# A decode kernel that streams its K and V: V beside a row's chain in halves, the row's kept K after eight of these V instead of sixteen, q spread at the chain's end

## The chip, the core and the metric

The kernel runs on one core of a Trainium2 chip. The metric is the device time of one execution in microseconds; below it is the median of three runs. One more execution was recorded by the hardware profiler, and all views of the profile are of that one.

## What is computed

A batch of 8 rows, one token each, 448 wide, goes twice through the same two blocks: an attention over a cache, then a small MLP. Both passes use the same weights and the same caches.

```
x = x + A(layernorm(x));  x = x + B(layernorm(x))     # pass 0
x = x + A(layernorm(x));  x = x + B(layernorm(x))     # pass 1

A(x):  q = x @ wq                    # 16 heads of 256; 8 heads of K and V, two q heads to each
       p = softmax(q k^T / 16)       # k, v: [8 rows, 8 heads, 4096, 256] bf16, read from HBM
       return (p v) @ wo
B(x):  h = gelu(layernorm(x) @ w1) ; shift by 1 or 2 tokens ; x1 = x + hs @ w2
       return x1 + gelu(layernorm(x1) @ w3) @ w4
```

With one token, the shift in B leaves zeros, so the product with w2 adds nothing, and the kernel leaves w1 and w2 out. K and V have 134 MB each, and each pass needs both; the second pass of a row needs its q, which depends on the whole first pass of that row.

## The kernel before

**Tiles and places.** Work on a row (batch element) is cut into four tasks, one for each pair of K/V heads (`gp` 0 to 3), and each task into four K chunks and four V chunks of 1 MB. A chunk lies in one of 15 places in SBUF (`NC = 15`, L61): 128 partitions of 8 KB, sixteen rows of 256 values in each. A task of pass `ps`, row `b` and heads `gp` is written `(ps, b, gp)` in the code, and an item is a task, 0 or 1 for K or V, and a chunk number.

**Kept chunks.** Chunks that both passes of a row use are kept where possible (`kept`, L64): for the heads in `keep` (gp 2 and 3), all eight K chunks (already transposed by pass 0) and four V chunks stay in their places from pass 0 to pass 1 of the row; one more V chunk (`inner`) and a quarter of another (`part`) wait in PSUM. So while a row stands between its two passes, twelve of the fifteen places are taken, and three are free to stream through.

**Per chunk.** A K chunk is transposed by VectorE (`transpose_k`, L751) and then scored on TensorE (`scores`, L766; two chunks of a pair are scored together when the first comes up, if they are in place); ScalarE makes the exponentials of two chunks (`exps`, L775). `transpose_p` (L802) and `spread_p` (L900) bring them into the form that PV wants. A V chunk takes 16 matmuls (`pv`, L819), one for each of the 16 rows y of a partition; they read the place in the order of y, so the first eight read its first half.

**The chain.** When the last V of a row's pass 0 has been used, what follows for that row is a chain of small dependent steps (`chain`, L494): copy o out of PSUM (`half`, L467), turn it (L473), product with wo (L365), norm (L227 to L302, with matmul L235 and a power on GpSimd, L254), product with w3 (L383), gelu (L400 to L405), product with w4 (L365), norm, product with wq (L316), q (L325). A chain is a Python generator; each `yield` is a place at which other work may be put. `step(idx)` takes the next piece of every open chain. It is called ahead of an item's matmuls and behind them, and for V of the tasks in `saved` once more between the eighth and the ninth matmul (`between`).

**Spread.** Before K of a row can be scored, its q has to be spread into one of two block-diagonal tiles (`spread_q`: four matmuls L335, four casts L339). That is done when the first K item of a row and pass comes up and no tile holds its q.

**Order.** All instructions are issued in the order of a list of items that `block` and `first_kept` (L553, L569) write by hand before anything is emitted. `due` holds V items that are owed; each K item is followed by one of them. Around a chain the list reads: the row's last kept heads in pass 0; then the V of the saved tasks (`units`), by themselves, while the chain of the row goes on; then K of the row's pass 1, kept heads first. For the first six chains there are four saved tasks, so sixteen V; for the last two only two, so eight V.

**Loads.** `emit_loads` (L698) runs behind every item. It takes the next chunk of `loads` (the items in order, without those that are kept) as long as a place is free, and issues one DMA on SP's queue: 1 MB at L738, or two neighbouring K chunks as 2 MB at L713. SP issues in order; each DMA waits until the place's last reader is done (PE for V, PE for K that has been scored). The very last chunk is the only one that comes in two halves (L741).

Of the kernel before, what the change touches and what calls it, by code (L numbers as in the profile page):

```python
# [17 lines left out]
def kernel(  # L18
# [161 lines left out]
    qbds = [consts.tile([128, 8, GP, 4, 2], BF16, name=f"qbd{k}") for k in range(2)]  # L180
    for t in qbds:
        nc.vector.memset(t[:].rearrange("p n g a h -> p (n g a h)"), 0.0)
    q_of = [None] * len(qbds)
# [144 lines left out]
    def spread_q(qT, qbd):  # L328


        qs = misc[0:32, 128 : 128 + 4 * NB2].rearrange("p (e n) -> p e n", e=4)
        for ep in range(4):
            e2, par = ep // 2, ep % 2
            sel = identb[:, 64 * e2 : 64 * e2 + 64].rearrange("p (j r) -> p r j", r=2)[:, par, :]
            nc.tensor.matmul(qs[:, ep, :], sel, qT, start=True, stop=True)  # L335
        yield
        for a in range(4):
            u = a // 2
            nc.vector.tensor_copy(  # L339
                qbd[32 * a : 32 * a + 32, :, :, a, :],  # L340
                qs.rearrange("p e (f g u h) -> p (e f) u g h", f=2, u=2, h=2)[:, :, u],
            )
# [151 lines left out]
    def chain(b, st, ready):  # L494
        OT = work.tile([128, 2, Hq // 2, 1], BF16, tag="OTb", bufs=1)
        yield from half(st["o", 1], st["z"], 1, OT[:, :, :, 0], ready)
        yield from add_cols(
            y_room(1)[:, 1],
            lambda i: OT[:, i % 2, i // 2 - Hq // 2],
            wo_sb,  # L500
            range(NB2 // 2, NB2),
            2,
        )
        xs = xT[:, :, b : b + 1]
        nc.vector.tensor_add(xs, xs, y_room(1)[:, 1])
        yield from mlp(b, 1)
        qT = chn.tile([128, NB2], BF16, tag="qT2", bufs=2)
        yield from project_q(b, 1, qT[:].unsqueeze(2))
        state[1, b] = {"qT": qT}

    def first_last(b, st, ready):

# [35 lines left out]
        ahead.append(units)  # L548

    tasks, items, due = [], [], []  # L550
    number = {}

    def block(k, v=None):  # L553

        fresh = [(number[v], 1, c) for c in range(4)] if v else []
        if k is None:
            items.extend(due + fresh)
            due.clear()
            return
        number[k] = len(tasks)  # L560
        tasks.append(k)
        for c in range(4):
            items.append((number[k], 0, c))
            items.extend(due[:1])
            del due[:1]
            if c == 0:
                due.extend(fresh)

    def first_kept(b, units, before):  # L569

        k2, k3 = ((0, b, gp) for gp in keep)
        todo = list(units)
        block(todo.pop(0), before)
        if len(todo) > 2:
            block(todo.pop(0))
        block(k2)
        block(todo.pop(0), k2) if todo else block(None, k2)
        block(k3)
        block(todo.pop(0), k3) if todo else block(None, k3)
        assert not todo  # L580
        for u in units:
            block(None, u)

    block((0, 0, free[0]))
    block((0, 0, free[1]), (0, 0, free[0]))
# [112 lines left out]
    def emit_loads(most=None):  # L698
        n = 0
        while loads and places and n != most:  # L700
            it = loads[0]
            both = both_for(it)
            if both:
                p, mate = both
                if p not in places or p + 1 not in places:
                    break
                for i, q in ((it, p), (mate, p + 1)):
                    loads.remove(i)
                    places.remove(q)
                    del held[i]  # L710
                    taken(i, q)
                _, b, gp = tasks[it[0]]
                nc.sync.dma_start(  # L713
                    places_t[:, p * PB : (p + 2) * PB],
                    A_k_cache[b, 2 * gp : 2 * gp + 2]
                    .rearrange("g s d -> (g s) d")
                    .rearrange("(p u z) d -> u p (z d)", u=2, z=32)[it[2] // 2],
                )
                n += 1
                continue  # L720
            p = place_for(it)
            if p is None:
                break
            del loads[0]
            taken(it, p)
            t, kv, c = it
            _, b, gp = tasks[t]
            dst = slots[p]
            rows = (A_v_cache if kv else A_k_cache)[b, 2 * gp : 2 * gp + 2].rearrange(
                "g s d -> (g s) d"  # L730
            )
            if kv:
                src = rows.rearrange("(a p y) d -> a p (y d)", a=4, y=16)[c]
            else:
                src = rows.rearrange("(p x y) d -> x p (y d)", x=4, y=16)[c]
            if loads:
                z0 = Q4 if tasks[t][0] == 1 and halfway(it) else 0
                nc.sync.dma_start(dst[:, z0:], src[:, z0:])  # L738
            else:
                for y in range(2):  # L740
                    nc.sync.dma_start(  # L741
                        dst[:, 8 * Dh * y : 8 * Dh * (y + 1)], src[:, 8 * Dh * y : 8 * Dh * (y + 1)]
                    )
            n += 1
# [117 lines left out]
    def run(g):  # L862
        while True:
            try:
                next(g)
            except StopIteration as e:
                return e.value
# [6 lines left out]
    def step(idx):  # L874

        for kind in ("chain", "last", "rest"):
            e = next((e for e in gens if e["kind"] == kind), None)
            if e is None:
                continue
            if not e["of"] or e["n"] < e["of"] * (idx - e["at"] + 1) / max(e["until"] - e["at"], 1):  # L880
                e["n"] += 1
                if next(e["g"], gens) is gens:
                    gens.remove(e)

    free_slots = list(range(NP))
    slot_of, ring_of = {}, {}
    v_items = [it for it in items if it[1] == 1]
# [16 lines left out]
    for idx, it in enumerate(items):  # L904
# [17 lines left out]
        if kv == 0:  # L922
# [5 lines left out]
                    state[0, b] = {}  # L928
            st = state[ps, b]
            if (ps, b) not in q_of:  # L930

                def next_use(k):
                    return next((m for m in range(n, len(tasks)) if tasks[m][:2] == q_of[k]), 999)

                k = max(range(len(qbds)), key=next_use)
                q_of[k] = (ps, b)
                run(spread_q(st["qT"][:] if ps == 1 else qT1[:, :, b], qbds[k]))
            qbd = qbds[q_of.index((ps, b))]
            if "z" not in st:
                z_t = chn.tile([128, 2, GP], FP32, tag="zall", bufs=4)  # L940
# [29 lines left out]
        else:  # L970
# [9 lines left out]
            if final and gp in free:  # L980
                pv_cols(oc, slot, c, gp, psv[slot_of[n]])
                if c % 2 == 1:

                    u = c // 2
                    scale_o(oc, rz_gp, gp, u, OT2[:, :, :, b])
                    h0 = 8 * gp + 4 * u
                    run(
                        add_cols(
                            st["y"],
                            lambda i: OT2[:, i % 2, i // 2, MID:],  # L990
                            wo_sb,
                            range(h0, h0 + 4),
                            4,
                            open=(claim(st), gp == free[-1] and u == 1),
                        )
                    )
            else:
                g8 = gp // 2
                if ("o", g8) not in st:
                    while len(in_use) == 2:  # L1000
                        step(10 * len(items))
                    st["o", g8] = next(t for t in o_banks if all(t is not u for u in in_use))
                    in_use.append(st["o", g8])
                if c == 0 and pairs_done.get((ps, b), 0) % 2 == 1:
                    done = pairs_done[ps, b] + 1

                    def ready(k=(ps, b), done=done):
                        return pairs_done[k] >= done

                    if ps == 0:  # L1010
                        g = (first_half if done == 2 else chain)(b, st, ready)
                        add_gen("chain", g)
                    elif done == 2:
                        add_gen("chain" if final else "last", first_last(b, st, ready))
                    else:
                        add_gen("last", last(b, st, ready))
                calm = tasks[n] in saved
                pv(st["o", g8], slot, c, gp, ring_of[it], (lambda: step(idx)) if calm else None)
                if ps == 0 and inside(it):
                    away(slot)  # L1020
                if ps == 0 and halfway(it):
                    nc.vector.transpose(store[4][:].bitcast(U32), slot[:, 0:Q4].bitcast(U32))
# [83 lines left out]
```

## Time and profile before

| | |
|---|---|
| median of three runs | 1136.0 us (1134.33 to 1137.39) |
| the profiled execution | 1138.53 us, span 1136.7 us |
| DMA | 438.25 MB, mean 386 GB/s |
| PE matmul busy | 652.4 us (57%) |
| DVE busy | 605.1 us (53%) |
| ACT busy | 164.0 us (14%) |
| PV, L819 | 3968 matmuls, 236.8 us |
| scores, L766 | 5376 matmuls, 252.2 us |
| transposes of K, L751 | 576, 457.7 us |
| V loads of 1,024 KB | 207, median 8.8 us from issue to landing |

PE is TensorE, DVE VectorE, ACT ScalarE, POOL GpSimd, SP the engine that issues the DMAs; "SPq" is its queue. The slices of the profile are fortieths of the span, 28.4 us each. A wait line names who waited and for whom, then the total in us, how often, and the longest. A timeline line gives start and length in us, engine, line and operation, and in brackets the idle time ahead of it and what ended that. "The chain that ended last" in the profile is the path of waits that led to the last instruction; it is not the row's chain of the section above.

### The profile page before, as it was taken

How to read it: one execution, taken by the hardware profiler on the slowest of the kernel's cores; microseconds unless marked ns; L12 is line 12 of the kernel's file. 1: busy time of each engine (PE TensorE's matmuls, PEld its weight loads, DVE VectorE, ACT ScalarE, POOL GpSimd, SP SyncE). 2: the span in 40 equal slices, each digit the busy share in tenths (PEclk: the TensorE clock that was granted, in tenths of full speed). 3: DMA queues.
4: the chain of work that ended last, by engine and by line, in shares of the span. 5: the costliest groups of instructions: out<-in, count | busy, mean ns of one | idle time of the engine just before them, and what ended most of it. 6: DMA issues, size and time to landing. Idle time of an engine off the chain costs nothing.

```text
span 1136.7 us, 30536 instructions
## 1 busy us (share of the span) xinstructions
PE 652.4 (57%) x13748; PEld 421.3 (37%) x13748; DVE 605.1 (53%) x1242; ACT 164.0 (14%) x610; POOL 16.3 (1%) x27
## 2 busy tenths in 40 slices
PE   3234476734757357564575555664466646865875
PEld 2122244512434235332353323442243424543654
DVE  4248730687306972268623685138741574476272
ACT  0011110211102111121101211011110111111020
POOL 0000000000000000000000000000000000000000
PEclk9985555756556555565555655556555655566565
DMA  9999999999999999899998999999999799999994
GB/s 357 397 424 428 423 392 340 368 425 417 365 365 397 423 396 364 326 427 421 419 337 321 428 423 409 359 356 428 421 402 362 313 423 418 348 424 421 358 396 200
DMA packets 56386, 438.25 MB, mean 386 GB/s; under 512 B 5944, under 2 KB 9920, under 8 KB 11712
## 3 DMA queue, kind: packets, MB, share of 16 engines
q1 hardware_dynamic: 56064, 435.93, 95.5%
q8 instruction: 107, 1.75, 0.6%
q10 hardware_dynamic: 192, 0.38, 0.1%
q14 instruction: 23, 0.19, 0.0%
HBM read 436.28 MB, written 0.01 MB: 384 GB/s over the span
## 4 chain that ended last, share of the span: by engine, by line
DMA 54%; PE 23%; DVE 15%; SPq 3%; issue 2%; ACT 1%; POOL 1%; DVEq 0%; ACTq 0%
DMA places<-in_A_v_cache_dram 35%; DMA places<-in_A_k_cache_dram 19%; DVE places L751 11%; PE sc L766 9%; PE o L819 7%; PE misc L365 3%; SPq L174 2%; PE misc L316 2%; DVE store L786 1%; PE misc L473 1%; DVE qbd L339 1%; SPq L738 1%; ACT p_n L775 1%; DMA wq_sb<-in_A_wq_dram 1%; POOL t L254 1%
## 5 line engine op out<-in xcount | busy, mean ns | idle before, releaser
L751 DVE STREAM_TRANSPOSE places<-places 128x512 uint32<-128x512 uint32 (+1 forms) x576 | 457.7, 854 | 100.0 <-DMA places<-in_A_k_cache_dram 98.2
L766 PE MATMUL sc<-places,qbd 128*8 128x128 bf16 (+1 forms) x5376 | 252.2, 339 | 247.0 <-DVE places L751 227.9
L819 PE MATMUL o<-places,ptw 128*8 128x256 bf16 x3968 | 236.8, 384 | 176.9 <-DMA places<-in_A_v_cache_dram 142.3
L766 PEld LDWEIGHTS <-qbd 128*8 128x8 bf16 x5376 | 135.2, 104 | 324.2 <-DVE places L751 163.7
L819 PEld LDWEIGHTS <-ptw 128*8 128x8 bf16 x3968 | 105.8, 104 | 246.1 <-issue 148.3
L775 ACT ACTIVATE p_n<-sc 128x256 bf16<-128x256 f32 x128 | 94.8, 741 | 369.5 <-PE sc L766 369.5
L900 ACT COPY ptw<-psv 128x32 bf16<-128x32 bf16 x248 | 50.9, 225 | 216.9 <-PE o L819 215.7
L468 DVE MEMSET o<- 128x256 f32 x31 | 8.4, 272 | 96.8 <-ACT o_sb L467 52.6
L440 DVE RECIPROCAL rz<-misc 128x8 f32<-128x8 f32 (+1 forms) x33 | 6.6, 201 | 97.2 <-PE misc L437 82.6
L809 ACT CAST psv<-misc 128x128 bf16<-128x128 f32 x64 | 17.0, 265 | 242.4 <-PE misc L802 239.8
L316 PEld LDWEIGHTS <-wq_sb 128*128 128x128 bf16 x1152 | 33.9, 104 | 26.5 <-issue 16.8
L473 PE MATMUL misc<-R,o_sb 128*128 128x8 f32 x124 | 28.7, 342 | 23.7 <-DVE qbd L339 13.3
L365 PEld LDWEIGHTS <-wo_sb 128*128 128x128 bf16 x1280 | 36.9, 104 | 10.3 <-issue 10.2
L473 PEld LDWEIGHTS misc<-R,o_sb 128*128 128x128 f32 x124 | 26.1, 292 | 33.9 <-ACT o_sb L467 19.9
L316 PE MATMUL misc<-xb,wq_sb 128*128 128x1 bf16 x1024 | 31.9, 166 | 7.0 <-DVE xb L283 6.8
L775 ACT ACTIVATION_READ_ACCUMULATOR p_n<-sc 128x1 f32 x128 | 33.7, 263 | 0.0
L254 POOL TENSOR_TENSOR t<-t,nhalf 128x2 f32<-128x2 f32 (+2 forms) x20 | 14.0, 703 | 1108.2 <-DVE t L275 1108.2
L365 PE MATMUL misc<-OT,wo_sb 128*128 128x1 bf16 x1024 | 29.8, 166 | 0.0
L339 DVE CAST qbd<-misc 32x64 bf16<-32x64 f32 x92 | 19.7, 214 | 16.5 <-PE misc L335 15.6
L793 DVE STREAM_TRANSPOSE places<-store 128x512 uint32<-128x512 uint32 x32 | 20.1, 685 | 12.0 <-PE sc L766 12.0
L467 ACT COPY o_sb<-o 128x256 f32<-128x256 f32 x31 | 11.5, 372 | 95.9 <-PE o L819 95.9
L325 DVE CAST qT<-misc 128x32 bf16<-128x32 f32 x8 | 1.5, 192 | 39.2 <-PE misc L316 39.2
(104 smaller groups left out, 308.3 us busy)
## 6 DMA issues: line engine op xcount, KB each, us to landing
places<-in_A_v_cache_dram SPq DMA_DIRECT2D x207, 1024.0 KB, 8.8
places<-in_A_k_cache_dram SPq DMA_DIRECT2D x54, 2048.0 KB, 20.5
places<-in_A_k_cache_dram SPq DMA_DIRECT2D x84, 1024.0 KB, 12.3
places<-in_A_v_cache_dram SPq DMA_DIRECT2D x8, 768.0 KB, 6.3
wo_sb<-in_A_wo_dram SPq DMA_DIRECT2D x1, 3584.0 KB, 28.4
wq_sb<-in_A_wq_dram SPq DMA_DIRECT2D x3, 1024.0 KB, 8.6
w_sb<-in_B_w_dram SPq DMA_DIRECT2D x1, 1568.0 KB
w_sb<-in_B_w_dram SPq DMA_DIRECT2D x3, 448.0 KB, 18.9
```

The source lines that it names most:

```text
L174: nc.sync.dma_start(t[:, fc * cols : (fc + 1) * cols], src[fc * 128 : fc * 128 + 128, :])
L254: nc.gpsimd.tensor_tensor(rs[:, k0:k1].rearrange("p n b -> p (n b)"), ve[:, k0:k1].rearrange("p n b -> p (n b)"), nhalf[:].to_broadcast([1 ...
L316: nc.tensor.matmul(q_ps[:, j * Hq + h, :], w, xbs(nb)[:, xi, :], start=(fc == 0), stop=(fc == 3),)
L339: nc.vector.tensor_copy(qbd[32 * a : 32 * a + 32, :, :, a, :], qs.rearrange("p e (f g u h) -> p (e f) u g h", f=2, u=2, h=2)[:, :, u],)
L365: nc.tensor.matmul(y_ps[:, fc, :], w[:, i, at : at + 128], rhs(i), start=start, stop=stop, skip_group_check=open is not None,)
L473: nc.tensor.matmul(ot_ps[:, j], o_sb[:].rearrange("p (i j) -> p j i", j=2)[:, j], R[:], start=True, stop=True)
L751: nc.vector.transpose(w, w)
L766: nc.tensor.matmul(sc[32 * k : 32 * k + 8, 128 * x : 128 * (x + nx)], qbd[:, ep, gp].rearrange("p a h -> p (a h)"), v, start=(n == 0), sto ...
L775: nc.scalar.activation(p_sb[:, :, :, 2 * u : 2 * u + 2].rearrange("p t i x -> p x t i"), sc[:, 256 * u : 256 * u + 256].rearrange("p (x t ...
L793: nc.vector.transpose(slot[:].bitcast(U32)[:, 512 * n : 512 * n + 512], store[n][:].bitcast(U32))
L819: nc.tensor.matmul(o_ps[32 * q : 32 * q + 8, :], ptz[:, at : at + 8], v[:, y * Dh : (y + 1) * Dh], start=False, stop=(y >= 12), skip_group ...
L900: nc.scalar.copy(ptw[:, ring_of[it], :, 6:8], psv[slot_of[it[0]]][:, it[2]])
```

## The change

Three things are done. In `first_kept`, the V of the saved tasks no longer stand by themselves: they are put into `due`, the first eight (`AFTER`) follow at once, and the rest alternate with the K items that come next, which are the kept K of the row's pass 1. The first eleven of these V are `narrow`: their load is issued as two DMAs of 512 KB, one for each half of the place, and between the eighth and ninth matmul of their PV two steps of the chain are taken; other V take none there any more. And `chain` ends with `give_q`, which spreads the row's new q at once, into the tile whose q is used again latest, counted from the next K item.

```diff
@@ chain
         yield from project_q(b, 1, qT[:].unsqueeze(2))
         state[1, b] = {"qT": qT}
+        give_q((1, b))
@@ the list of items
-    number = {}
+    number, narrow = {}, set()
+    AFTER = 8
     def block(k, v=None):
         fresh = [(number[v], 1, c) for c in range(4)] if v else []
         if k is None:
-            items.extend(due + fresh)
+            due.extend(fresh)
+            items.extend(due)
             due.clear()
             return
@@ first_kept
         assert not todo
+        items.extend(due)
+        due.clear()
         for u in units:
-            block(None, u)
+            due.extend((number[u], 1, c) for c in range(4))
+        narrow.update(due[: AFTER + 3])
+        items.extend(due[:AFTER])
+        del due[:AFTER]
@@ emit_loads
-            if loads:
+            if loads and it not in narrow:
                 z0 = Q4 if tasks[t][0] == 1 and halfway(it) else 0
                 nc.sync.dma_start(dst[:, z0:], src[:, z0:])
             else:
                 for y in range(2):
                     nc.sync.dma_start(
                         dst[:, 8 * Dh * y : 8 * Dh * (y + 1)], src[:, 8 * Dh * y : 8 * Dh * (y + 1)]
                     )
@@ behind step
+    def give_q(who):
+        here = next((i[0] for i in items[now[0] :] if i[1] == 0), 0)
+        def next_use(k):
+            return next((m for m in range(here, len(tasks)) if tasks[m][:2] == q_of[k]), 999)
+        k = max(range(len(qbds)), key=next_use)
+        q_of[k] = who
+        run(spread_q(state[who]["qT"][:] if who[0] == 1 else qT1[:, :, who[1]], qbds[k]))
@@ the loop over items, K
             if (ps, b) not in q_of:
-                def next_use(k):
-                    return next((m for m in range(n, len(tasks)) if tasks[m][:2] == q_of[k]), 999)
-                k = max(range(len(qbds)), key=next_use)
-                q_of[k] = (ps, b)
-                run(spread_q(st["qT"][:] if ps == 1 else qT1[:, :, b], qbds[k]))
+                give_q((ps, b))
@@ the loop over items, V
-                calm = tasks[n] in saved
-                pv(st["o", g8], slot, c, gp, ring_of[it], (lambda: step(idx)) if calm else None)
+                pv(st["o", g8], slot, c, gp, ring_of[it],
+                    (lambda: (step(idx), step(idx))) if it in narrow else None)
```

More of the change, by code (lines that the diff above doesn't have):

```diff
@@ L1016 @@
                         add_gen("last", last(b, st, ready))
-                calm = tasks[n] in saved
-                pv(st["o", g8], slot, c, gp, ring_of[it], (lambda: step(idx)) if calm else None)
+                pv(
+                    st["o", g8],
+                    slot,
+                    c,
+                    gp,
+                    ring_of[it],
+                    (lambda: (step(idx), step(idx))) if it in narrow else None,
+                )
                 if ps == 0 and inside(it):
```

## The prediction

> **What bounds it now.** I read the page's forty slices first, then the shares of the chain that ended last, then the waits of SP's queue, then the stages around one row's chain in the windows view.
>
> ```profile
> PE   3234476734757357564575555664466646865875
> ...
> DMA  9999999999999999899998999999999799999994
> GB/s 357 397 424 428 423 392 340 368 425 417 365 365 397 423 396 364 326 427 421 419 337 321 428 423 409 359 356 428 421 402 362 313 423 418 348 424 421 358 396 200
> ...
> DMA 54%; PE 23%; DVE 15%; SPq 3%; issue 2%; ACT 1%; POOL 1%; DVEq 0%; ACTq 0%
> ```
>
> The DMA row says nine tenths nearly everywhere, but the rate swings between about 425 and 320 GB/s, in dips that come once per row. So the kernel is bound by its transfers (438.25 MB), and the time to be won is in the dips. Windows, with columns length, busy us (count) of PE, weight load, DVE, ACT, POOL, then clock, DMA share and GB/s:
>
> ```profile
> 429.20:452.30 23.10, 19.01 (x434) 14.17 (x438) 5.47 (x32) 2.21 (x10) 1.25 (x2) 0.50 0.96 354
> 452.30:477.00 24.70, 11.60 (x162) 6.95 (x150) 2.23 (x11) 2.34 (x10) 0.00 (x0) 0.50 0.95 367
> 477.00:487.00 10.00, 8.22 (x209) 5.70 (x212) 7.98 (x13) 2.61 (x9) 0.00 (x0) 0.50 0.71 274
> 900.00:950.00 50.00, 25.17 (x538) 14.58 (x530) 37.12 (x56) 8.14 (x30) 0.00 (x0) 0.60 1.01 423
> ```
>
> The last line is a K stretch without trouble: 423 GB/s, which I take as full rate. The first is a row's chain, from the copy of its last o (L467) to its q (L325): PE is busy 19 of 23 us, and 23.1 x (1 - 354/423) = 3.8 us of transfer are lost. The second is the rest of the sixteen V: PE is busy less than half, nothing else works, and still 3.3 us are lost. The third begins at the first score of the kept K: 3.5 us lost.
>
> Why the V stretch loses, with PE idle, is in the waits of SP's queue and in PE's timeline (start, length, what, idle before it):
>
> ```profile
> SPq L738 <- DMA places<-in_A_v_cache_dram: 195.1, 121, 7.0
> SPq L738 <- PE o L819: 167.3, 123, 3.8
> SPq L738 <- PE sc L766: 153.9, 59, 9.3
> ```
> ```profile
> 447.09 1.16 PE L316 MATMUL misc<-xb,wq_sb 128*128 128x1 bf16 x32 [1.00 <-DVE xb L283]
> 448.18 0.60 PE L819 MATMUL o<-places,ptw 128*8 128x256 bf16 x8
> ...
> 473.32 1.02 PE L819 MATMUL o<-places,ptw 128*8 128x256 bf16 x16 [2.49 <-DMA places<-in_A_v_cache_dram]
> 474.13 0.31 PE L335 MATMUL misc<-qT,identb 128*32 128x32 bf16 x4
> 476.10 0.99 PE L473 MATMUL misc<-R,o_sb 128*128 128x8 f32 x4 [1.66 <-DVE qbd L339]
> 477.02 1.88 PE L766 MATMUL sc<-places,qbd 128*8 128x256 bf16 x32
> ```
>
> Twelve of the fifteen places hold what pass 1 will use again, so V runs through three places, and SP can ask for V n+3 only when PV has read V n. PE waits for V, V waits for SP, SP waits for PE: a ring with three members. Then, at 474, the kept K wait for q to be spread (L335, four casts L339, PE idle 1.66), and only their scores free further places: the 3.5 us hole.
>
> Lost per stage, by length x (1 - rate/423) from the same view: for the six rows with sixteen V, chains 2.8, 4.2, 3.8, 3.2, 2.9, 2.8 (sum 19.5; 22.0 to 24.4 us long); rest of V 5.1, 3.3, 3.3, 6.0, 4.4, 3.6 (25.7); first 10 us of kept K 1.8, 1.9, 3.5, 3.4, 2.2, 5.8 (18.6). That is **10.6 us a row, 7.4 of it behind the chain**. The two rows with eight V (chains from 959.6 and 1052.8) lose 2.2 + 3.0 and 3.4 + 2.7.
>
> **The change, part by part.** Sums go against the profiled execution (span 1136.7, time 1138.53, 2.5 above the median of the runs, 1136.0); I take the difference from the median.
>
> *Kept K after eight V.* Nothing is added or removed: the order of V is the same, and eight kept K items move in front of the last eight V of six rows, alternating with them. Each pair of kept K scored frees two places (1.88 us of PE per pair of scores, no transfer, no transpose), so from there on places are freed at twice the rate. The ring of three is opened, and the last eight V (a transfer each of 1,024 KB, 2.5 us at 423 GB/s) are asked for well ahead. On SP these requests stand in the order in which places come free; the first after the narrow V waits for one pair of scores and one PV. The last narrow V is asked for some 25 us after the chain's start, the next request comes about 4.5 us later (half() L473 1.0 with 0.5 of waiting, scores 1.9, PV 1.0), while three V in flight are 7.4 us of work and a request needs about 2 us to flow (issue at 479.02, the 4-us stretch after it back at full rate from 481). So the 7.4 us fall to between 0 and 3; I take 1.0, since transfers end on their slowest queue and not all together. If that cover is gone (PE later by over 3 us), each us is lost once per row, 6 us in all.
>
> *q spread at the chain's end.* Four matmuls (0.31) and four casts (0.88) move out of the stretch where PE idles 1.66 us for them into the V; there the next PV covers the casts. It is part of the 3.5 us hole and is not counted twice. The number of spreads stays 23.
>
> *Halves and the chain.* Now three steps of the chain per V (before it, between its eighth and ninth matmul, after it); then four, two of them in the middle. By the new order PE alternates one PV half, one piece of chain, with twelve halves (six V) up to the spread, where 7.5 V stand in the 23.1 us now. Pieces, from PE's timeline: L473 1.02, L365 1.86, L235 0.59, L383 1.80, L365 1.81, L235 0.56, L437 0.60, L316 about 3.9: 12.1. Twelve halves at 0.55 (0.60 alone, 1.02 the two): 6.6. Waits, each less the half that covers it: copy of o 0.5; end of L365 to L235 0.9 - 0.55 = 0.35; L235 to L383 1.8 - 0.55 = 1.25 (DVE, then POOL 0.70, then DVE); L383 to L365 1.1 - 0.55 = 0.55; again 0.25; L235 to L316 2.0 - 0.55 = 1.4: 4.3. **Sum 23.0, what it is now**: the waits for V (0.66, 1.26, 0.61 in the row shown) go, but a half hides less of DVE's and POOL's latency than a whole PV. The last two V add 2.1 and the spread 0.3: 25.4 us for eight V. DMA meanwhile: what was asked for before the chain lasts until 435.5, that is 6.3 us; twelve halves at 1.27 are 15.2. Lost 25.4 - 21.5 = 3.9, and writing the refills out one by one, each 2 us behind its half, the uneven requests (long gaps at the two norms) make it 4.7. Bounds: 2 if the refill of the first half gains more than a piece of chain, 8 if the chain takes 3 us more. So the chain's own loss does not fall: 3.3 now, **4.7 then**. The gain is all behind it.
>
> *The price of halves.* 6 x 11 + 2 x 8 = 82 V are split: 82 more requests (0.33 us each on SP, which is waiting anyway) and packets of 4,096 B for 8,192. In the packet records of before the last V, the one split today, has 256 packets of median 159 ns; an 8,192 B packet takes 309. So 8 x (318 - 309) = 0.07 us a V, 0.8 a row. Above, 0.7 us a half if each began on an idle queue (packets after a pause take about 1,000 ns); below nothing. I take 0.8, as requests overlap in a ring of six.
>
> The Trainium skill speaks against this part: "DMA: Bandwidth & Descriptors", sections "Measured" and "Rules for kernel authors", asks for at least 1 MiB per transfer, and its fit (section "Anatomy of one DMA") puts about 2.0 us on each transfer whatever its size; an estimate from that page would be 82 x 2 = 164 us more if nothing overlapped. The trace has 1 MiB transfers in a row at 423 GB/s, so the fixed part is covered with several in flight.
>
> *PV without a step in the middle* for the other V: moves pieces of work by one PV, in stretches where PE waits for DMA; nothing. Weight loads fall by 288 pairs (nine more pairs of chunks lie side by side), beside other work: nothing.
>
> *Sum.* Row with sixteen V: 4.7 + 0.8 + 1.0 = 6.5 for 10.6, so -4.1; six rows -24.6. Row with eight: 4.7 + 0.6 + 0.8 = 6.1 for 5.65 on average; two rows +0.9. Together -24: **1112 us**.
>
> **Rivals.**
> (A) *Little gain.* The chain with two pieces between halves runs 2 us longer and DMA starves through it: 6.7 + 0.8 + 2 = 9.5 a row: -6.6, +7: about 1135. For it: PE is busy 19 of 23 us, at a granted clock of 0.50. Against: PE's waits for V vanish.
> (B) *Halves also mend the chain.* Requests half a V earlier keep DMA going: 2 + 0.8 + 0.5 = 3.3 a row, -44, and -5: 1088. For: SP's 167 us of waiting for PE o. Against: PE's own 23 us.
> (C) *Slower.* Place: the narrow V. Mechanism: each half is a transfer of its own and starts late on queues that have run dry, 0.35 us a half (half of the 0.7 above). 164 x 0.35 = 57 us: 1169. It decides from 24/164 = 0.15 us a half. For: starts after a pause are seen all through the dips. Against: six in flight.
> (D) *The halves do nothing*, because a refill waits for the whole PV. The built program's waits say otherwise: a half's refill waits for the eighth matmul.
>
> **Chances.** Forecast (1098 to 1125) 0.62, A 0.15, B 0.14, C 0.08, D 0.01. The range takes in B and most of the way to A: 1089 to 1131. A measurement of this kernel tells 0.3% (3.4 us) from no change: faster 0.87, same 0.05, slower 0.08.
>
> **What will show it.** Windows behind the chains at 400 GB/s and more, and the slices' dips half as long; the chains still 22 to 24 us with a lower rate than now (about 340); no 1.66 us before L473 after the casts of qbd; half V transfers landing in under 8 us. Wrong if the chain windows exceed 25 us, if the K stretches after it fall below 415 GB/s, or if the SP waits for half V grow past what the whole V cost.

## The result, and the profile after

The changed kernel takes 1128.15 us (median of four runs, 1127.98 to 1129.88) against 1136.22 us (median of four runs of the kernel before): a ratio of 0.9934, interval 0.9917 to 0.9951. It is faster by 8 us, a third of the 24 that were forecast; the time lies inside the range, near its slow end. The profiled execution has a span of 1126.2 us for 1136.7.

The same parts of the page as shown of before, now of the changed kernel (slices of 28.2 us, then the shares of the chain that ended last, then the V transfers with count, size and median time to landing):

```profile
GB/s 360 396 425 427 423 363 331 421 425 419 344 366 425 422 412 337 402 424 423 404 325 424 425 425 389 333 426 423 422 355 352 422 422 377 333 425 416 302 420 202
...
DMA 63%; PE 20%; DVE 9%; SPq 3%; issue 2%; POOL 1%; ACT 1%; DVEq 0%; ACTq 0%
...
places<-in_A_v_cache_dram SPq DMA_DIRECT2D x125, 1024.0 KB, 18.0
...
places<-in_A_v_cache_dram SPq DMA_DIRECT2D x166, 512.0 KB, 6.8
```

The dips are narrower and just as deep: in the six long rows their lowest slices are 331, 344, 337, 325, 333 and 352, where 340, 365, 326, 321, 356 and 313 stood. In the two rows with eight V they are deeper, 333 and 302 for 348 and 358. Next the windows view of the changed kernel, one long row (a row with sixteen V: chain, then up to the first kept K, then 12 us from there) and then the first row with eight V, cut alike:

```profile
425.60:447.90 22.30, 17.70 (x410) 12.69 (x411) 5.61 (x32) 1.70 (x8) 1.25 (x2) 0.55 0.92 337
447.90:451.50 3.60, 3.11 (x52) 2.45 (x47) 1.17 (x6) 0.82 (x3) 0.00 (x0) 0.50 0.86 313
451.50:463.50 12.00, 7.21 (x181) 4.29 (x180) 2.95 (x7) 2.55 (x9) 0.00 (x0) 0.78 1.00 379
944.50:967.00 22.50, 18.15 (x410) 12.99 (x411) 5.63 (x32) 1.65 (x8) 1.25 (x2) 0.50 0.86 303
967.00:970.60 3.60, 3.11 (x52) 2.45 (x48) 1.16 (x6) 0.59 (x2) 0.00 (x0) 0.50 0.65 198
970.60:982.60 12.00, 9.38 (x201) 5.95 (x204) 8.20 (x12) 3.50 (x12) 0.00 (x0) 0.50 0.99 406
```

The 25 us of V by themselves are gone: 3.6 us stand between chain and first kept K. But the chain, about as long as before, has fallen from 354 to 337 GB/s, and in the row with eight V from 380 to 303, with 198 behind it. The chain of that row before:

```profile
959.60:981.10 21.50, 19.03 (x434) 14.14 (x438) 5.47 (x32) 2.02 (x9) 1.25 (x2) 0.50 0.99 380
```

SP's waits in the changed kernel (L749 asks for halves, L746 for whole chunks):

```profile
SPq L749 <- PE o L827: 137.0, 101, 2.8
...
SPq L746 <- PE sc L774: 79.3, 33, 3.8
...
SPq L746 <- DMA places<-in_A_v_cache_dram: 68.4, 42, 4.0
SPq L746 <- PE o L827: 42.1, 44, 5.1
...
SPq L749 <- DMA places<-in_A_v_cache_dram: 27.9, 19, 4.7
```

Waiting for earlier V to land fell from 195 to 96 us (68.4 and 27.9); waiting for PE's PV, 167 before, is 179 now (137.0 and 42.1). So PE's PV is now the wait that holds most of the V requests back.

For the comparisons below I count the lost time from the packet records: each packet of 4, 8 and 16 KB at its usual duration (159, 309 and 611 ns, within 3 ns of the medians), smaller ones by their size, summed and divided by sixteen queues, taken off the length of a stretch. That keeps the dearer small packets out of it. For before it gives 3.4 (chain), 4.3 (to the first kept K) and 3.3 (12 us from there) in a mean long row.

| run | us | V in the chain | chain | to K | 12 us from K | long row | rows with eight V |
|---|---|---|---|---|---|---|---|
| before | 1136.2 | 7.5 | 3.4 | 4.3 | 3.3 | 10.9 | 5.4, 6.3 |
| the change | 1128.2 | 6 | 4.6 | 1.2 | 1.6 | 7.3 | 8.5, 7.8 |
| e1 order only | 1114.3 | 7.5 | 3.0 | 1.1 | 3.3 | 7.3 | 5.3, 7.5 |
| e2 old order | 1148.4 | 6 | 4.7 | 3.8 | 2.8 | 11.3 | 7.3, 7.6 |
| e3 one step | 1102.5 | 7.5 | 1.0 | 0.6 | 3.3 | 4.9 | 4.0, 4.4 |
| e4 whole loads | 1127.2 | 6 | 6.1 | 1.8 | 0.7 | 8.6 | 8.3, 9.1 |
| e5 two in the middle | 1109.6 | 7.5 | 1.8 | 0.4 | 3.2 | 5.4 | 5.4, 5.5 |
| e6 one step, late q | 1107.4 | 7.5 | 1.7 | 0.5 | 3.4 | 5.6 | 3.7, 4.3 |
| e7 one step, whole | 1110.6 | 7.5 | 2.9 | 0.7 | 3.1 | 6.7 | 4.8, 8.5 |
| e8 long rows alone | 1121.8 | 6 | 4.5 | 1.4 | 1.4 | 7.3 | 4.6, 7.3 |
| e9 nine V | 1098.5 | 7.5 | 1.4 | 0.8 | 2.0 | 4.2 | 3.0, 4.2 |
| e10 ten V | 1099.4 | 7.5 | 1.1 | 0.7 | 1.5 | 3.2 | 5.0, 4.4 |
| e11 all in halves | 1110.6 | 7.5 | 1.1 | 0.4 | 4.0 | 5.5 | 3.1, 4.7 |

"V in the chain" is how many PV stand between the copy of o (L467) and q (L325) in a long row. The losses are of each run's one profiled execution, the times medians of four. The whole packet time at the usual durations is about 1030 us before and 6 more with the change. The losses can be summed over the eight rows: with the change they are 17 us less, packets add 6, and the two profiled spans differ by 10.5. A loss can move from one stage of a row to the next, so rows are safer to compare than stages.

Each ratio below is to runs of the kernel before that were made beside it, with medians from 1133.7 to 1137.5 us; for e9, e10 and e11 it was 1137.5.

### The profile page after: what moved, and what is told of

It reads as the page before. It is cut to its first block, busy times and chain, and to the rows that moved or that the text cites. A ratio compares the mean times of both kernels' runs of the same rounds, so it can differ in the third digit from the quotient of the medians.

```text
span 1126.2 us, 30082 instructions
## 1 busy us (share of the span) xinstructions
PE 650.9 (58%) x13460; PEld 418.5 (37%) x13460; DVE 607.6 (54%) x1242; ACT 163.6 (15%) x610; POOL 16.3 (1%) x27
## 4 chain that ended last, share of the span: by engine, by line
DMA 63%; PE 20%; DVE 9%; SPq 3%; issue 2%; POOL 1%; ACT 1%; DVEq 0%; ACTq 0%
DMA places<-in_A_v_cache_dram 40%; DMA places<-in_A_k_cache_dram 22%; PE o L827 6%; PE sc L774 5%; DVE places L759 4%; PE misc L316 3%; PE misc L365 3%; SPq L174 2%; DVE store L794 2%; PE misc L383 1%; POOL t L254 1%; SPq L746 1%; PE misc L235 1%; PE misc L473 1%; DMA wq_sb<-in_A_wq_dram 1%
## 5 line engine op out<-in xcount | busy, mean ns | idle before, releaser
L774 PE MATMUL sc<-places,qbd 128*8 128x256 bf16 (+1 forms) x5088 | 249.7, 349 | 220.0 <-DVE places L759 207.5
L827 PE MATMUL o<-places,ptw 128*8 128x256 bf16 x3968 | 242.8, 381 | 151.2 <-DMA places<-in_A_v_cache_dram 129.0
L774 PEld LDWEIGHTS <-qbd 128*8 128x8 bf16 x5088 | 132.4, 105 | 292.3 <-issue 120.6
L365 PEld LDWEIGHTS <-wo_sb 128*128 128x128 bf16 x1280 | 39.2, 104 | 35.0 <-issue 34.9
L316 PEld LDWEIGHTS <-wq_sb 128*128 128x128 bf16 x1152 | 34.7, 104 | 32.1 <-issue 21.7
L316 PE MATMUL misc<-xb,wq_sb 128*128 128x1 bf16 x1024 | 33.2, 165 | 11.5 <-DVE xb L283 8.9
L473 PE MATMUL misc<-R,o_sb 128*128 128x8 f32 x124 | 28.2, 338 | 19.7 <-ACT o_sb L467 11.9
L473 PEld LDWEIGHTS misc<-R,o_sb 128*128 128x128 f32 x124 | 25.5, 286 | 31.4 <-ACT o_sb L467 22.9
L383 PE MATMUL misc<-xb,w_sb 128*128 128x1 bf16 (+1 forms) x560 | 18.8, 166 | 11.8 <-DVE xb L283 9.4
L383 PEld LDWEIGHTS <-w_sb 128*128 128x128 bf16 x560 | 17.9, 105 | 19.4 <-issue 18.6
```

Source lines behind the costliest of these rows:

```text
L316: nc.tensor.matmul(q_ps[:, j * Hq + h, :], w, xbs(nb)[:, xi, :], start=(fc == 0), stop=(fc == 3),)
L365: nc.tensor.matmul(y_ps[:, fc, :], w[:, i, at : at + 128], rhs(i), start=start, stop=stop, skip_group_check=open is not None,)
L383: nc.tensor.matmul(h_ps[:, c * nb : c * nb + nb], w, xbs(nb)[:, xi, :], start=(fc == 0), stop=(fc == 3),)
L473: nc.tensor.matmul(ot_ps[:, j], o_sb[:].rearrange("p (i j) -> p j i", j=2)[:, j], R[:], start=True, stop=True)
L774: nc.tensor.matmul(sc[32 * k : 32 * k + 8, 128 * x : 128 * (x + nx)], qbd[:, ep, gp].rearrange("p a h -> p (a h)"), v, start=(n == 0), sto ...
L827: nc.tensor.matmul(o_ps[32 * q : 32 * q + 8, :], ptz[:, at : at + 8], v[:, y * Dh : (y + 1) * Dh], start=False, stop=(y >= 12), skip_group ...
```

## The experiments

**e1: the order alone.** Of the change, only the list of items is kept.

```diff
-            if loads and it not in narrow:
+            if loads:
@@ chain
-        give_q((1, b))
@@ pv
-                    (lambda: (step(idx), step(idx))) if it in narrow else None,
+                    (lambda: step(idx)) if tasks[n] in saved else None,
```

> Only the order of the items is that of the change (kept K after eight V); V come whole, one step of the chain stands in the middle of a PV as before, q is spread when the first K comes up. Theory 1 (the order is all of the gain; two steps between halves make PE end fewer V in the chain, the halves cost 6 us of packets and more in the two rows with eight V): chain windows lose 3.3 us as before, the stage behind them 3 to 4 instead of 7.4, the short rows as before: 1110 to 1118 us, faster than the whole change. Theory 2 (the halves are needed to feed the ring of three): 1126 us or more. Theory 3 (the early spread of q is what closes the hole): the hole at the first kept K stays 2 us or more a row, 1124 to 1130.

Measured: 1114.25 us, ratio 0.9824 (0.9810 to 0.9839). The order by itself brings 20 us, near the 24 forecast for the whole change, but by chance: a long row loses 3.0 us in the chain and 3.3 at the kept K, where 4.7 and 1.0 were put. What was added to it took 14 away. Theory 1 holds by the time and by the stretch up to the first kept K, where 1.1 us are lost for 4.3. The 12 us from the first kept K still lose 3.3, as before: the order alone does not close that hole. Halves and the early q do not either, since e3 has both and loses the same 3.3 there.

**e2: the order undone.**

```diff
-        items.extend(due[:AFTER])
-        del due[:AFTER]
+        items.extend(due)
+        due.clear()
```

> The change with its order undone: all sixteen V stand by themselves again, the first eleven in halves, two steps in the middle, q spread early. Theory 1: the V behind the chain lose 3 to 5 us a row again and the hole 2 to 3, and the dearer chain stays: 1134 to 1142 us. Theory 2 (halves bring the gain): 1128 or less. Theory 3 (early q brings it): 1120 to 1128.

Measured: 1148.43 us, 1.0121 (1.0104 to 1.0139). Halves, two steps and early q in the old order are 14 us slower than before, worse than theory 1 said. The windows of this run for the same row, chain and V behind it:

```profile
430.20:452.80 22.60, 18.21 (x410) 13.04 (x411) 5.64 (x32) 1.69 (x8) 1.25 (x2) 0.50 0.91 326
452.80:481.30 28.50, 13.46 (x186) 7.75 (x177) 2.19 (x11) 2.79 (x12) 0.00 (x0) 0.50 0.93 348
```

Both stages are below the 354 and 367 GB/s of before, and the second is 3.8 us longer: ten V stand behind the chain where 8.5 stood.

**e3: one step between the halves.**

```diff
-                    (lambda: (step(idx), step(idx))) if it in narrow else None,
+                    (lambda: step(idx)) if it in narrow else None,
```

> The change with one step of the chain between the halves instead of two. Theory 1 (PE sets the pace in the chain, and two pieces between halves put only six V into it where 7.5 were): the chain stays 22 to 24 us long, 7.5 V in it, its loss falls from 4.6 to about 3 us and the 1.2 us behind it go: 1112 to 1118 us. Rival (the chain is a string of latencies that steps cannot shorten, so one step makes it longer and q late): chain windows 25 us and more, 1126 to 1135.

Measured: 1102.46 us, 0.9717 (0.9702 to 0.9731): one step less in the middle is worth 26 us, more than the 10 to 16 expected. Its windows for the same row and for the row with eight V:

```profile
416.50:439.50 23.00, 18.84 (x434) 13.30 (x438) 5.46 (x32) 2.25 (x10) 1.25 (x2) 0.54 1.01 383
439.50:442.30 2.80, 1.71 (x24) 1.42 (x16) 1.15 (x6) 0.37 (x1) 0.00 (x0) 0.50 0.99 369
442.30:454.30 12.00, 7.60 (x217) 5.02 (x217) 3.07 (x7) 3.52 (x13) 0.00 (x0) 0.86 0.88 313
...
926.00:947.30 21.30, 18.77 (x434) 13.98 (x438) 5.48 (x32) 2.02 (x9) 1.25 (x2) 0.50 1.01 377
```

The second step in the middle did not shorten the chain: in the six long rows it takes 22.1 us on average here and 22.3 in the change. What differs is the count of matmuls, 434 against 410, that is 24 more PV matmuls, 1.5 V. From the chain's start to its end this run asks for 14 halves (at 1.4 to 21.0 us), the change for 11 (at 1.4 to 20.8), and so in all six long rows. Three halves are 3.8 us of transfer, 23 us in six rows if nothing of it were made up later. By the table the change loses 14 us more than this run in the long rows and 8 more in the two rows with eight V: 22 of the 26 measured.

**e4: whole loads, two steps.**

```diff
-            if loads and it not in narrow:
+            if loads:
```

> The change with every V loaded whole, still with two steps in the middle. Theory 1: packets of 4,096 B go (-6 us), but a refill now waits behind two pieces of the chain and the second half: 1.5 to 2 us more lost in each of eight chains: 1132 to 1138 us. Rival (halves are mere cost): 1118 to 1122 us, the short rows back at 5 to 6 us lost.

Measured: 1127.23 us, 0.9932 (0.9915 to 0.9948), the time of the change itself, between the ranges of the two theories and in neither. The chains lose 1.5 us more a row, as theory 1 had it, and the packets 6.6 us less in all; the two cancel. With two steps the halves are worth nothing.

**e5: three steps a V, two of them in the middle.**

```diff
         emit_loads()
-        step(idx)
+        if it not in narrow:
+            step(idx)
```

> The change with two steps between the halves, but none behind a narrow V's item: three steps a V as in the kernel before, two of them in the middle. Theory 1 (what costs is the number of V that PE ends while the chain lasts its fixed 22 us; three steps a V put 7 to 7.5 V there): 1102 to 1109 us, chains losing 1 to 2 us. Rival (two pieces in front of the second half are what delays the refills): 1118 to 1130 us, chains losing over 3 us.

Measured: 1109.61 us, 0.9772 (0.9738 to 0.9807), just above the range of theory 1, far from the rival. Of the 26 us, 19 go with the number of steps per V; 7 more go with their place: with two in the middle the chains lose 1.8 us instead of 1.0.

**e6: one step, q spread late.** The edit of e3, and:

```diff
-        give_q((1, b))
```

> One step between the halves, and q spread only when the first kept K comes up, as before. If the early spread matters, four matmuls and four casts stand again in front of the kept K, about 1.5 us a row in a stretch where DMA runs dry: 1108 to 1115 us against 1102.5. If it is covered (the kept K wait in PE behind half() anyway): within 3 us of 1102.5.

Measured: 1107.41 us, 0.9754 (0.9724 to 0.9785). That is 5 us more than e3, but the intervals of the two just overlap, and the stage that would have to show it (to K, 0.5 for 0.6 us) does not. What the table has instead, 1.7 us for 1.0, lies in the chain, ahead of the spread. Whether the early spread is worth 5 us or nothing stays open.

**e7: one step, whole loads.** The edits of e3 and e4 together.

> One step in the middle, q early, new order, but every V loaded whole. Theory 1: without halves the ring has three members of 1 MB; chains lose 3.0 us as in the run with the order alone instead of 1.0, less 0.8 us of packets a row: 1108 to 1114 us. Rival (halves are mere packet cost): 1096 to 1101 us.

Measured: 1110.63 us, 0.9783 (0.9752 to 0.9814). Chains lose 2.9 us for 1.0: halves are worth 8 us, packets paid, when one step stands in the middle; with two (e4) they were worth nothing. Theory 1 holds.

**e8: rows with eight V as before.**

```diff
-        narrow.update(due[: AFTER + 3])
+        if len(due) > AFTER:
+            narrow.update(due[: AFTER + 3])
@@ pv
-                    (lambda: (step(idx), step(idx))) if it in narrow else None,
+                    (lambda: (step(idx), step(idx))) if it in narrow
+                    else (lambda: step(idx)) if tasks[n] in saved else None,
```

> The change, but in the two rows with eight V everything as before (whole V, one step in the middle). Theory 1: the change loses 8.5 and 7.8 us in these rows where before lost 5.4 and 6.3, and pays 1.2 us of packets; undoing it there gives 5 to 6 us: 1121 to 1124 us. Rival (those rows are not the cause): 1127 to 1130.

Measured: 1121.84 us, 0.9881 (0.9848 to 0.9915): 6 us back from two rows, as theory 1 had it. SP's timeline of the changed kernel in the first of them shows where they were lost:

```profile
946.48 16.98 SPq L749 DMA_DIRECT2D places<-in_A_v_cache_dram  x10
967.37 0.33 SPq L746 DMA_DIRECT2D places<-in_A_v_cache_dram  x1
968.33 1.18 SPq L746 DMA_DIRECT2D places<-in_A_k_cache_dram  x2
```

Ten halves are asked for until 963.5, then nothing for 3.9 us. In these rows the eight V are all that is narrow; what refills their places (one V, two K) is whole and has to wait for the second half, with L316 standing between the halves. That whole refills matter here is read from this one timeline. The runs show that the two steps do: e3, with one step and the same refills, loses 4.0 and 4.4 us in these rows; e4, with two and whole loads throughout, 8.3 and 9.1.

**e9 and e10: nine and ten V in front of the kept K, with one step.** The edit of e3, and:

```diff
-    AFTER = 8
+    AFTER = 9      # e10: 10
```

> One step in the middle, and nine V in front of the first kept K instead of eight (twelve V in halves). In the run with eight the stage behind the chain still loses 3.3 us of each long row: the last half is asked for, then half() and the first scores and one PV stand on PE, 5 us without a request while four halves (5 us of work) are in flight. If this gap is the cause, a ninth V ahead of the scores asks for its refill before them: 1.0 to 1.5 us a row less, 1093 to 1098 us. Rival (what DMA lacks there is places, not requests in time, so one more V in the ring of three only prolongs it): 1102 to 1106.

> The same with ten V in front of the first kept K. If the gap is the cause, the gain of the ninth V is there already and the tenth adds little, 1093 to 1099 us; if the ring of three costs more with each V, 1104 to 1110.

Measured: 1098.50 us, 0.9659 (0.9615 to 0.9703), and 1099.40 us, 0.9679 (0.9632 to 0.9727). Both lie half a microsecond above the range given for the gap and well below that of the rival. The last loss of e3, 3.3 us in the 12 us from the first kept K, falls to 2.0 and 1.5. In PE's timeline of e3 it stands here:

```profile
441.42 0.99 PE L473 MATMUL misc<-R,o_sb 128*128 128x8 f32 x4 [1.09 <-DVE qbd L339]
442.34 1.02 PE L774 MATMUL sc<-places,qbd 128*8 128x256 bf16 x16
...
444.33 1.72 PE L827 MATMUL o<-places,ptw 128*8 128x256 bf16 x32
...
450.95 0.61 PE L827 MATMUL o<-places,ptw 128*8 128x256 bf16 x16 [3.43 <-DMA places<-in_A_v_cache_dram]
```

Behind the last half, PE does half() and the first scores before the PV that frees the next place; SP's next request comes 5.2 us after the last (445.44 after 440.28), and PE pays 3.43 us at 450.95. e9's ends overlap e3's interval by a hair, so its gain, 4 us by the medians and 6.6 by the ratios, is likely and not certain. Whether ten V are better than nine stays open. Both beat the change and the kernel before.

**e11: all sixteen V in halves, one step.** The edit of e3, and:

```diff
-        narrow.update(due[: AFTER + 3])
+        narrow.update(due)
```

> One step in the middle, eight V in front, and all sixteen V in halves, not the first eleven. The refill of the first V behind the scores is asked for half a PV earlier (0.5 us a row less), and five more V a row pay packets (0.4 us a row): within 3 us of 1102.5. If halves help wherever they stand: under 1099; if packets or requests cost more than 0.07 us a V: over 1106.

Measured: 1110.60 us, 0.9777 (0.9733 to 0.9821): 8 us slower than e3 by the medians, 7 by the ratios, in the range of the last of the three expectations but not for its reason. Packet time is 2.4 us more for 30 more V in halves, 0.08 each; the stage from K loses 4.0 us for 3.3 in each long row, about 4 in six. Why it does, and where the rest went, was not found.

## Why the prediction was wrong

**What bounds it, and the order**: right for the ring of three. The order alone took 20 us (e1), and undoing it cost as much (e2); the stage up to the first kept K fell from 4.3 to 1.2 us a row. The hole at the kept K was counted as closed too. With the change it loses 1.6 us for 3.3, but in e1 and e3 it stays at 3.3, and only nine or ten V in front of it (e9, e10) make it smaller while the chain loses little.

**q spread early**: counted at nothing of its own; e6 leaves 0 to 5 us open.

**Halves and the chain**: the sum for the chain's length was right. 23.0 us were worked out for the chain, and 21.4 to 22.6 measured in the long rows, with twelve halves up to the spread; the waits were put at 4.3. In PE's timeline of the row at 425.6 the three longest stand here:

```profile
432.59 1.05 PE L383 MATMUL misc<-xb,w_sb 128*128 128x1 bf16 x28 [0.88 <-DVE xb L283]
...
436.14 0.88 PE L365 MATMUL misc<-HT_t,w_sb 128*128 128x1 bf16 x28 [0.60 <-DVE HT_t L405]
...
439.75 0.60 PE L827 MATMUL o<-places,ptw 128*8 128x256 bf16 x8
441.46 1.16 PE L316 MATMUL misc<-xb,wq_sb 128*128 128x1 bf16 x32 [1.12 <-DVE xb L283]
```

The half hides 0.6 us of a latency and PE sits out the rest, as written: 0.47, 0.32, 0.88, 0.60, 0.32, 1.12 and 0.30, together 4.0 us.

**The step that failed** is the balance of transfers drawn from those six V. It has two mis-sized terms in a long row. The 4.7 us were for the 25.4 us up to the last of eight V; that stretch (chain and to K) loses 4.6 + 1.2 = 5.8. For the pause behind it I let "three V in flight", 7.4 us of work, be the cover, and took 1.0; it loses 1.6. SP's timeline of the row at 425.6 has the pause, 3.5 us without a request up to 454.58 (predicted 4.5):

```profile
424.71 27.08 SPq L749 DMA_DIRECT2D places<-in_A_v_cache_dram  x17
454.58 2.80 SPq L746 DMA_DIRECT2D places<-in_A_v_cache_dram  x4
```

So the pause was not longer than written (in the first long row alone it was, 6.5 us); the cover was thinner. In that row the chain's last three requests go out 14.8, 18.0 and 20.8 us into it, about 3 us apart for 1.3 us of transfer each. Counted from the packet records, one half is left in flight when q is there, at 22.3 (0.9 to 1.2 in the six long rows). PE then ends the last two V at once, and when the pause begins 3.6 to 4.6 halves are in flight, 4.6 to 5.8 us of work where six halves had been put. The prediction's own balance, 21.5 us of transfer for 25.4, already says that the ring runs low there, and the part on the pause counts it as full. Together 1.7 us a row more than predicted, or 1.3 against the 10.9 that the same count gives for before: 8 us in six rows.

**Rows with eight V**: the third mis-sized term. They were given the long rows' 4.7 and 0.8 (5.5) and measure 8.5 and 7.8: 5 us more. I had not asked what two steps between the halves do to these rows, where the next refills are whole; with one step (e3) they lose 4.0 and 4.4. With the 8 us of the long rows this is 13 of the 16 us between -24 and -8. The other 3 are the profiled executions, which differ by 10.5 us where the medians differ by 8.

**The price of halves**: right. 0.07 us a V was taken; the packet time rose by about 6 us for 82 V, 0.075 each. Rival C (0.35 us a half) is not seen: the packets of 512 KB transfers have the duration that was assumed, 159 ns, and with one step (e7 against e3) halves gain 8 us. The Trainium skill's fixed 2.0 us per transfer ("DMA: Bandwidth & Descriptors", section "Anatomy of one DMA") comes from a fit to transfers issued from GpSimd. SP issues the loads here, and no cost of that size shows: the losses and the packet time give 10.8 us between the two profiled spans, which differ by 10.5.

**The rivals.** A named the right place and the wrong reason: it had the chain 2 us longer, and the chain was not longer, only emptier of V. B, halves that mend the chain (its terms add up to 1087, not 1088), is nearest to e3, which has one step and not two. D fell with e7.

**The signs.** The chains came out as said, under 25 us and at 337 GB/s in the row shown; the 1.66 us ahead of L473 are gone, and half V land in 6.8 us. The sign that failed is the rate behind the chains: 400 GB/s and more was forecast, and the row shown has 313 and then 379. Of the signs of being wrong none came: the K stretches after it run at 423 to 425 GB/s in windows of 50 us and more, and SP's waits for half V are no longer than those for whole V were.

**What I left unpriced** is the cheaper neighbour. The change puts a fourth step into each V; I asked what four steps give and never what three would give with the same halves. By the terms of the prediction that is 7.5 V in the same 22.5 us, fifteen halves or 19 us of requests, with 6.3 us in flight ahead of them: more than the chain lasts. That is e3, and it is 26 us faster than the change.

## What to carry to other kernels

Where transfers are refilled by the engine that also does a chain of small steps, count the transfers asked for while the chain lasts: this chain did not get shorter by stepping it faster (22.3 us with four steps a V, 22.1 with three), it only took the V's turns away. Price a stretch together with the state in which it leaves the ring of buffers, because the dip comes a few microseconds behind the cause. And take a change of three parts apart before adding it up: here the order brought 20 us, the second step in the middle cost 26, and the halves paid or not depending on that step.

## What the runs showed of the hardware

Transfers of 512 KB were not dear: in the change 21,248 packets of 4,096 B belong to them, and packets of this size have a median of 159 ns, as the 256 of before had. The granted clock of TensorE was 0.50 to 0.56 in the chains of the change and of e3. In the 12 us behind one in e3 it was 0.86, with PE busy less, and there the same sixteen PV matmuls take 0.61 us where they take 1.03 in the chain.
